# Decode of two attention-and-MLP layers: the two halves of a head's score rows gathered in one bank, and the last query weights loaded first from two queues

## The chip, the cores and the metric

The kernel runs on one core of a Trainium2 chip. A core has a matrix engine (TensorE, PE in the profile, with its weight loads shown apart as PEld), a vector engine (VectorE, DVE), a scalar engine (ScalarE, ACT), a general one (GpSimd, POOL) and a queue engine (SyncE, SP), each with its own instruction stream, and 16 DMA engines that move data from the chip's main memory into its working memory (SBUF). PE writes into eight banks of accumulator memory (PSUM); DVE and ACT copy from there. The metric is the device time of one execution in microseconds, as the median of several executions; less is better.

## The reference

Eight rows x of 448 numbers, one per batch entry, go twice through an attention block A and an MLP block B, with the same caches and weights in both layers:

```python
x = x + _A_ref(_layernorm(x), A_k_cache, A_v_cache, A_wq, A_wo)
x = x + _B_ref(_layernorm(x), B_w1, B_w2, B_w3, B_w4)
x = x + _A_ref(_layernorm(x), A_k_cache, A_v_cache, A_wq, A_wo)
x = x + _B_ref(_layernorm(x), B_w1, B_w2, B_w3, B_w4)
```

In A, x times `wq` gives 16 query heads of 256 numbers; each of the 8 key-value heads serves two of them. For each batch entry and key-value head there are 4096 keys and 4096 values of 256 numbers in bf16 (2 MB each): scores q.k / 16, a softmax over the 4096 positions, the weighted sum of the values, and `wo` on the 16 results together. In B, a first part (`w1`, `w2`) shifts along a sequence of length one, so that nothing of it is left and x1 = x; the rest is x1 + gelu(layernorm(x1) w3) w4, with 1792 hidden numbers.

## The kernel before, in words

**Order of the work.** The whole program is written as a list of operations, each with an engine, a modelled duration, the keys that it reads and writes, the PSUM banks that it touches, and a priority. `Plan.schedule` (L156) places them one by one in modelled time: on each engine, among the operations that are ready, the one of lowest priority number. `Plan.synchronise` turns the dependences into semaphore waits, and each engine then runs its own list strictly in order. Where PE would stand idle in the model, `filler` (L1672) puts in matmuls that keep its clock up (L1679 in the profile). An operation with engine "ev" is an eviction that the schedule gives to DVE or ACT, whichever can take it first.

**Loads.** All loads but one result go out on SP's queue (`dma`, L623, and `load`, L649). SP's priorities are of their own: a load of keys or values has its running number 0, 1, 2, ..., and a weight load made by `dma_once` (L629) with `at` has 4 * at - 0.5. So `at = 0` goes ahead of all keys, and `at = 2` (7.5) behind the first eight quarters of key and value tiles. Keys and values pass through one buffer `kv` of 30 slots; a slot holds a quarter of a head's keys or values (512 KB), and adjacent free slots can be filled by one load of up to four quarters (2048 KB). SP waits until the operation that last read a slot is done (L643 in the waits of SP).

**Heads.** `front(layer, b, h)` makes the scores and the softmax of a head, `back(layer, b, h)` the weighted sum of values and the part of `wo`. In front, each quarter u of the keys that was loaded anew is transposed by PE in two pieces (`transpose_piece`, L1464; transposes at L1476) into one of four banks psT0 to psT3, which go round by `next_bank` and `tcount`, and copied back over its own slot by DVE (L1407) or ACT (L1408). Of the 8 key heads the five last, and some quarters of their values, stay in the buffer from the first layer to the second (`KEEP_K`), where their keys are not transposed again.

**Scores by rows.** 13 of the 16 head passes of a batch entry (7 of the first layer, 6 of the second; not the last head, nor the first one of the second layer) score "by rows": the queries, 32 columns, stand still in PE and the keys stream through it, 512 at a time. `score_rows` (L1365, matmuls at L1374) scores two quarters: four groups of 32 output rows, for the four half quarters, each in two passes c = 0, 1 over the even and odd elements of a head. `turn_rows` (L1383) copies that bank to a tile `sr` (512 columns in bf16, by DVE at L1387 or ACT at L1388), and four matmuls (L1398) turn it so that positions lie along partitions, and pick the two rows that belong to head h out of each group. This happens twice a head, for quarters 0 and 1 and for quarters 2 and 3, each time in a bank of its own and through the one tile `sr`. The other passes score with the keys as the stationary side (L1136). All scores of a head land in 64 columns of bank psM; then sS (L1204), the maximum (L1209, L1211, L1215), the exponential (L1221), the sum (L1225, L1227).

**The queries** lie in four tiles: `q1b` and `q2T`, two each (by the parity of b), for the first and the second layer, 16 columns for c = 0, 16 for c = 1 and 16 of zeros. The first layer's are made for all batch entries at the start by `first_queries` (L1558), 128 matmuls at L892 that need all of wq and wqx. The second layer's are made head by head, between one head's scores and the next one's, by `second_queries` (L1522, L892 and L1527), which use psM as well.

**Query weights.** `wq` has 448 rows. Three loads of 128 rows each (1024 KB) fill `wq_sb`. Of the last 64 rows, columns 0 to 2047 go to partitions 0 to 63 of `wqx_sb`, and columns 2048 to 4095 to partitions 64 to 127, with a load of 256 KB each.

**Around it.** `mid` (L1506) runs the MLP of one row between the layers and makes the first queries of the second layer; the heads of the first layer for the next batch entry run beside it. For one batch entry (`MLP_ROW`, b = 5) `with_first_results` lends one of the four psT banks to an MLP of six rows. The last quarters of the last head's keys in the first layer stay in the four psT banks until the second layer takes them (`hold`, `held_banks`).

Of the kernel before, what the change touches and what calls it, by code (L numbers as in the profile page):

```python
# [6 lines left out]
P = 128  # L7
B = 8
D = 448
HKV = 8  # L10
DH = 256
# [461 lines left out]
def bass_interleave_layers__gqa_block_cached__mixer_s_mlp__decode_kernel(  # L473
# [43 lines left out]
    w4_sb = sb("w4_sb", [P, 14 * D], bf)  # L517
    ident_f = sb("ident_f", [P, P], f32)
    ident_b = ident_f[:, :].bitcast(bf)[:, 1:2 * P:2]
    xT = sb("xT", [P, NC5, B], bf)  # L520

# [10 lines left out]
    ymk = acc[0]  # L532
    cs_q = sb("cs_q", [P, 32], f32)
    cs_h = sb("cs_h", [P, 14], f32)
# [9 lines left out]
    kh = sb("kh", [P, 1024], bf)  # L544
    q2T = [sb(f"q2T{i}", [P, 48], bf) for i in range(2)]
    cursor[0] = (cursor[0] + 31) // 32 * 32
# [22 lines left out]
    x_row = over("x_row", [B, NC5 * P], bf, w4_sb)  # L569
    NR, NO, NS = 6, 2, 2  # L570
    pT = [sb(f"pT{i}", [P, 32, 2], bf) for i in range(NR)]
    pm = [sb(f"pm{i}", [P, 2], f32) for i in range(NS)]
# [7 lines left out]

    sS = [sb(f"sS{i}", [P, 64], bf) for i in range(NS)]
    oS = sb("oS", [P, 2, DH], bf)
    o_last = over("o_last", [P, G], bf, oS)
# [507 lines left out]
    done = {}  # L1091

    def first_q(b, prio):
        for c in range(2):
            dv(lambda v, c=c: v.tensor_copy(
                q1b[b % 2][:, 16 * c:16 * c + 16].rearrange("p (h j) -> p h j", j=2),
                psM[:, Q1 + b:Q1 + 32 * B:B].rearrange("p (h j c) -> p h c j", j=2, c=2)[:, :, c, :]),
               rd=["q1"], wr=[("q1b", b % 2, c)], banks=[M], prio=prio)

    def front(layer, b, h, prio=None):  # L1100
# [8 lines left out]
        if layer == 0:  # L1109
            def rhs(c):  # L1110
                return q1b[b % 2][:, 16 * c + 2 * h:16 * c + 2 * h + 2]
            qall = q1b[b % 2]
            qk = [("q1b", b % 2, 0), ("q1b", b % 2, 1)]
        else:
            def rhs(c):
                return q2T[b % 2][:, 16 * c + 2 * h:16 * c + 2 * h + 2]
            qall = q2T[b % 2]
            qk = [("q2", b % 2, h)]
        ks = dict(kept_k)
        fresh = [u for u in range(4) if u not in ks and not (layer and h == HALF)]  # L1120
# [30 lines left out]
        for u in range(4):  # L1151
# [79 lines left out]
    def back(layer, b, h):  # L1231
# [132 lines left out]

    def score_rows(qs, qall, keys, prio):  # L1365


        bank = next_bank()

        def mm(t):  # L1370
            last = None
            for c in range(2):
                for g in range(4):
                    last = t.matmul(psT[bank][32 * g:32 * g + 32, :], qall[:, 16 * c:16 * c + 32],  # L1374
                                    slot_ap(qs[g // 2], g % 2 * 1024, 1024)[:, c:1024:2], start=(c == 0),
                                    stop=(c == 1), skip_group_check=True, tile_position=(0, 32 * g))
            return last
        o = plan.op("pe", mm, (0.47, 0.92, 1024, 8), "scr", rd=keys, wr=[("psT", bank)],
                    banks=[("T", bank)], prio=prio and prio + len(plan.ops))
        o.tbank = bank  # L1380
        return o

    def turn_rows(half, h, bank, par, prio):  # L1383

        def ev(e):
            if e is nc.vector:
# [3 lines left out]
                prio=prio and prio + len(plan.ops)).tbank = bank  # L1390

        picks = ident_b.rearrange("p (g c) -> p g c", g=4)[:, :, 2 * h:2 * h + 2]

        def mm(t):
            last = None
            for k in range(4):
                a = SB + 32 * half + 8 * k
                last = t.matmul(psM[:, a:a + 8], sr[:, k * P:(k + 1) * P], picks, start=True, stop=True)  # L1398
            return last
        plan.op("pe", mm, (0.17, 0.17, 32, 4), "scturn", rd=SR + ["ident_f"],  # L1400
                wr=[("sc", par, x) for x in range(2 * half, 4)], banks=[M], prio=prio and prio + len(plan.ops))

# [119 lines left out]
    def second_queries(b, h, prio):  # L1522

        q, src = q2T[b % 2], x2c[b % 2]
        pe(lambda t: q_mms(t, range(4 * h, 4 * h + 4), lambda kc: src[:, kc, 0:1], psM, SC,
                           1, QW), 16, rd=[("x2", b)] + WQ, wr=["psM"], banks=[M], prio=prio, width=QW)
        dv(lambda v: v.scalar_tensor_tensor(  # L1527
            q[:, 0:32].rearrange("p (c x) -> p c x", c=2)[:, :, 2 * h:2 * h + 2],
            cs_q[:, 4 * h:4 * h + 4].rearrange("p (c j) -> p c j", c=2), mom2[b % 2][:, 2:3],
# [209 lines left out]
```

## Time and profile before

| | |
|---|---|
| median of 3 executions | 1093.52 us (1092.39 to 1094.42) |
| the profiled execution, its own time | 1095.86 us |
| its span, first to last instruction | 1094.1 us |
| mean granted PE clock | 0.933 |
| busy: PE, DVE, ACT, POOL | 948.4, 665.9, 335.0, 98.0 us |
| read from main memory | 434.18 MB, 397 GB/s over the span |

The profile is that of one execution. Its span leaves out what lies before the first and after the last instruction, here 1.8 us. "Busy" counts an engine's instructions; what an engine waited for stands in the lists of waits. Lines such as L1387 are those of the listing above.

### The profile page before, as it was taken

The page shows a single profiled execution, that of the slowest core. Times are in us where ns is not written, and L with a number is a line of the kernel's source. Part 1 is how long each engine was busy: PE and PEld are TensorE (multiplying, and loading weights), DVE is VectorE, ACT ScalarE, POOL GpSimd, SP SyncE. Part 2 cuts the span into 40 slices and gives each one's busy share as a digit, 9 for nine tenths or more (in the row PEclk, how much of TensorE's full clock was granted, in tenths as well). Part 3 has the DMA queues.
Part 4 walks back from the last instruction along what each step waited for, and adds up shares of the span by engine and source line. Part 5 has one row for each costly group of instructions (what it writes and reads, how often), then busy time and mean ns, then how long its engine had stood idle before and what let it go on. Part 6 is the DMA issues. An engine that isn't in the chain of part 4 may idle for free.

```text
span 1094.1 us, 34653 instructions
## 1 busy us (share of the span) xinstructions
PE 948.4 (87%) x15414; PEld 636.6 (58%) x15414; DVE 665.9 (61%) x2004; ACT 335.0 (31%) x935; POOL 98.0 (9%) x281
## 2 busy tenths in 40 slices
PE   4889888898988989888988889888898998999886
PEld 3556555565556655666556565566555765566554
DVE  3457445675656756666567675667555765566565
ACT  0234123341334303343133322334133440343131
POOL 0001000010100101011010101001010000111010
PEclk9899899997999969999799998999899997999896
DMA  9999999999999999999999999999999999999892
GB/s 333 409 424 421 391 403 425 426 418 375 410 424 427 412 390 392 425 424 415 372 425 425 424 404 390 425 425 420 398 380 427 424 417 381 396 426 410 310 412 120
DMA packets 60417, 436.43 MB, mean 399 GB/s; under 512 B 6494, under 2 KB 9708, under 8 KB 39276
## 3 DMA queue, kind: packets, MB, share of 16 engines
q1 hardware_dynamic: 60260, 434.22, 97.5%
q8 instruction: 121, 1.98, 0.7%
q14 instruction: 28, 0.23, 0.1%
q10 hardware_dynamic: 8, 0.00, 0.0%
HBM read 434.18 MB, written 0.01 MB: 397 GB/s over the span
## 4 chain that ended last, share of the span: by engine, by line
DMA 57%; PE 31%; DVE 6%; ACT 2%; issue 2%; SPq 1%; POOL 0%; POOLq 0%; DVEq 0%
DMA kv<-in_A_v_cache_dram 39%; DMA kv<-in_A_k_cache_dram 15%; PE psT L1476 8%; PE psP L1257 8%; PE psT L1374 4%; PE psM L1136 3%; PE psR L1307 2%; PE psM L892 2%; DMA wqx_sb<-in_A_wq_dram 2%; DMA w_sb<-in_B_w_dram 1%; PE psM L1054 1%; DVE kv L1407 1%; ACT pT L1221 1%; SPq L626 1%; ACT kv L1408 1%
## 5 line engine op out<-in xcount | busy, mean ns | idle before, releaser
L1476 PE MATMUL psT<-ident_f,kv 128*128 128x128 f32 x2752 | 391.5, 283 | 27.0 <-DMA kv<-in_A_k_cache_dram 25.0
L1476 PEld LDWEIGHTS psT<-ident_f,kv 128*128 128x128 f32 x2752 | 296.7, 142 | 111.8 <-issue 69.6
L1407 DVE COPY kv<-psT 128x512 f32<-128x512 f32 x388 | 265.7, 690 | 135.3 <-PE psT L1476 131.4
L1408 ACT COPY kv<-psT 128x512 f32<-128x512 f32 x332 | 193.3, 586 | 437.3 <-PE psT L1476 340.1
L1257 PE MATMUL psP<-kv,pT 128*2 128x256 bf16 x4096 | 185.8, 293 | 36.4 <-DMA kv<-in_A_v_cache_dram 28.8
L1387 DVE CAST sr<-psT 128x512 bf16<-128x512 f32 x157 | 108.4, 691 | 73.6 <-PE psT L1374 60.2
L1257 PEld LDWEIGHTS psP<-kv,pT 128*2 128x2 bf16 x4096 | 76.1, 82 | 90.0 <-DMA kv<-in_A_v_cache_dram 44.3
L1211 POOL PARTITION_ALL_REDUCE gm<-pm x128 | 45.4, 355 | 773.2 <-DVE pm L1209 768.4
L1374 PE MATMUL psT<-kv,q1b 128*32 128x512 bf16 x896 | 72.5, 394 | 17.9 <-ACT kv L1408 14.9
L1221 ACT ACTIVATE pT<-sS,nb,fac 128x32 bf16<-128x32 bf16 x128 | 52.6, 417 | 106.9 <-DVE nb L1215 106.9
L1271 DVE CAST oS<-psP 128x256 bf16<-128x256 f32 x128 | 53.7, 419 | 45.8 <-PE psP L1257 45.3
L1307 PE MATMUL psR<-wo_sb,oT 128*1 128x448 bf16 x444 | 67.4, 387 | 3.5 <-DVE oT L1287 3.1
L1225 POOL PARTITION_ALL_REDUCE Db<-rs x128 | 51.0, 398 | 195.3 <-ACT pT L1221 195.3
L1374 PE MATMUL psT<-kv,q2T 128*32 128x512 bf16 x768 | 60.3, 397 | 3.4 <-DVE kv L1407 2.0
L1398 PEld LDWEIGHTS psM<-ident_f,sr 128*128 128x128 bf16 x832 | 42.5, 97 | 30.7 <-DVE sr L1387 16.5
L1398 PE MATMUL psM<-ident_f,sr 128*128 128x8 bf16 x832 | 52.4, 170 | 7.9 <-DVE sr L1387 6.5
L1221 ACT ACTIVATE pT<-sS,nb 128x32 bf16<-128x32 bf16 x128 | 40.8, 326 | 57.7 <-DVE nb L1215 57.6
L1273 DVE TENSOR_TENSOR oS<-psP,oS 128x256 bf16<-128x256 f32 x128 | 54.2, 424 | 3.5
L1281 PEld LDWEIGHTS psP<-sel,oS 128*128 128x128 bf16 x512 | 24.4, 99 | 39.5 <-DVE oS L1273 29.2
L1204 DVE CAST sS<-psM 128x64 bf16<-128x64 f32 x128 | 27.8, 217 | 29.5 <-PE psM L1136 20.2
L1281 PE MATMUL psP<-sel,oS 128*128 128x2 bf16 x512 | 32.2, 167 | 14.1 <-DVE oS L1273 13.3
L1388 ACT CAST sr<-psT 128x512 bf16<-128x512 f32 x51 | 29.8, 585 | 42.2 <-PE psT L1374 37.9
(197 smaller groups left out, 853.0 us busy)
## 6 DMA issues: line engine op xcount, KB each, us to landing
kv<-in_A_k_cache_dram SPq DMA_DIRECT2D x69, 2048.0 KB, 20.8
kv<-in_A_v_cache_dram SPq DMA_DIRECT2D x53, 2048.0 KB, 17.8
kv<-in_A_v_cache_dram SPq DMA_DIRECT2D x187, 512.0 KB, 7.5
kv<-in_A_v_cache_dram SPq DMA_DIRECT2D x21, 1024.0 KB, 11.1
kv<-in_A_k_cache_dram SPq DMA_DIRECT2D x40, 512.0 KB, 8.1
kv<-in_A_k_cache_dram SPq DMA_DIRECT2D x10, 1536.0 KB, 15.6
kv<-in_A_v_cache_dram SPq DMA_DIRECT2D x5, 1536.0 KB, 12.2
wo_sb<-in_A_wo_dram SPq DMA_DIRECT2D x1, 3584.0 KB, 45.6
```

The costliest lines, as they stand in the source:

```text
L1221: return a.activation(pT[nr][:, :, :].rearrange("p i j -> p j i")[:, jj, :], sview[:, jj, :], ACT.Exp, bias=nb[nm][:, jj:jj + 1], scale=sc ...
L1257: last = t.matmul(ps[g4:g4 + 2, PV0:PV0 + DH], pT[nr][:, k, :], slot_ap(q, s * 256, 256), start=(i < 4), stop=(i >= 28), skip_group_check= ...
L1271: plan.op("dve", lambda v: v.tensor_copy(oS[:, 0, :], po), 0.36, "o", rd=[("pv", par, x) for x in range(4)], wr=["oS0"], banks=[bk], prio=hi)
L1273: plan.op("dve", lambda v: v.tensor_tensor(oS[:, 1, :], po, oS[:, 0, :], ALU.subtract), 0.36, "o", rd=["oS0"] + [("pv", par, x) for x in r ...
L1281: last = t.matmul(ps[:, PV1 + 2 * c:PV1 + 2 * c + 2], oS[:, w, c:DH:2], sel[:, :], start=(w == 0), stop=(w == 1))
L1307: last = t.matmul(psR[r:r + 1, 0:D], oT[no][:, i % 2, i // 2:i // 2 + 1], wo_sb[:, a:a + D], start=(k == 1 and i < 2), stop=(k == turn_at ...
L1374: last = t.matmul(psT[bank][32 * g:32 * g + 32, :], qall[:, 16 * c:16 * c + 32], slot_ap(qs[g // 2], g % 2 * 1024, 1024)[:, c:1024:2], sta ...
L1387: return e.tensor_copy(sr[:, :], psT[bank][:, :])
L1398: last = t.matmul(psM[:, a:a + 8], sr[:, k * P:(k + 1) * P], picks, start=True, stop=True)
L1407: return e.tensor_copy(dst, psT[bank][:, :])
L1408: return e.copy(dst, psT[bank][:, :])
L1476: last = t.transpose(psT[bank][:, s * P:(s + 1) * P], src, ident_f[:, :])
```

## The change

Two edits stand in one diff, and the tiles move a little for them.

**One copy a head.** The four query tiles become one tile `qz` of 272 columns: for each layer and each parity of b 64 columns, in which 16 zeros, the 16 queries of c = 0, 16 zeros and the 16 queries of c = 1 follow each other, with 16 zeros at the end. A window of 32 columns that begins at the queries of c holds them in its first 16 columns and zeros in the others; a window that begins 16 columns earlier holds the zeros first. So the first half of a head's keys scores into the upper 16 rows of each group of 32, and adds zero to the lower ones; the second half the other way round, in the same bank. The bank is taken before the first half (`held_banks.add`), kept out of the round of banks meanwhile, and given back with the one copy that follows the second half. The four turning matmuls then pick four columns of each group, 16 in all, instead of two.

**The wqx loads.** The load for partitions 0 to 63 gets `at = 0.05` (priority -0.3), behind x and ahead of the first keys, on SP; the one for partitions 64 to 127 is issued by ACT, as its first operation. The wq loads keep their place. Both need semaphores of their own, as before.

```diff
+    qz = sb("qz", [P, 272], bf)
...
-    q1b = [sb(f"q1b{i}", [P, 48], bf) for i in range(2)]
-    q2T = [sb(f"q2T{i}", [P, 48], bf) for i in range(2)]
...
-        for q in q1b + q2T:
-            gp.memset(q[:, :], 0.0)
+        gp.memset(qz[:, :], 0.0)
...
+    def at_q(layer, b, c):
+
+        return 128 * layer + 64 * (b % 2) + 16 + 32 * c
...
-                o = score_rows([ks[u - 1], ks[u]], qall, qk + full + [("s", ks[u - 1], 0), ("s", ks[u - 1], 1)], prio)
-                turn_rows(u // 2, h, o.tbank, par, prio)
+                if u == 1:
+                    rbank = next_bank()
+                    held_banks.add(rbank)
+                o = score_rows([ks[u - 1], ks[u]], u // 2, lambda c, half: at_q(layer, b, c) - 16 * half, rbank,
+                               qk + full + [("s", ks[u - 1], 0), ("s", ks[u - 1], 1)], prio)
+                if u == 3:
+                    turn_rows(h, rbank, par, prio)
...
-                    k = 16 * (u // 2) + 4 * (s % 4) + 2 * (u % 2) + s // 4 if in_rows else i
+                    k = 8 * (s % 4) + 4 * (u // 2) + 2 * (u % 2) + s // 4 if in_rows else i
...
-    def score_rows(qs, qall, keys, prio):
-        bank = next_bank()
+    def score_rows(qs, half, window, bank, keys, prio):
...
             for c in range(2):
+                a = window(c, half)
                 for g in range(4):
-                    last = t.matmul(psT[bank][32 * g:32 * g + 32, :], qall[:, 16 * c:16 * c + 32],
-                                    slot_ap(qs[g // 2], g % 2 * 1024, 1024)[:, c:1024:2], start=(c == 0),
-                                    stop=(c == 1), skip_group_check=True, tile_position=(0, 32 * g))
+                    last = t.matmul(psT[bank][32 * g:32 * g + 32, :], qz[:, a:a + 32],
+                                    slot_ap(qs[g // 2], g % 2 * 1024, 1024)[:, c:1024:2],
+                                    start=(half == 0 and c == 0), stop=(half == 1 and c == 1),
+                                    skip_group_check=True, tile_position=(0, 32 * g))
...
-        o.tbank = bank
+        if half == 0:
+            o.tbank = bank
...
-    def turn_rows(half, h, bank, par, prio):
+    def turn_rows(h, bank, par, prio):
...
-        picks = ident_b.rearrange("p (g c) -> p g c", g=4)[:, :, 2 * h:2 * h + 2]
+        held_banks.remove(bank)
+        picks = ident_b.rearrange("p (g a x) -> p a g x", g=4, a=2)[:, :, :, 2 * h:2 * h + 2]
...
-                a = SB + 32 * half + 8 * k
-                last = t.matmul(psM[:, a:a + 8], sr[:, k * P:(k + 1) * P], picks, start=True, stop=True)
+                a = SB + 16 * k
+                last = t.matmul(psM[:, a:a + 16], sr[:, k * P:(k + 1) * P], picks, start=True, stop=True)
...
-        dma_once("wqx", [(wqx_sb[0:64, :], A_wq[384:D, 0:2048], 1 << 19),
-                         (wqx_sb[64:P, :], A_wq[384:D, 2048:4096], 1 << 19)], ["wqx0", "wqx1"], 2)
+        dma_once("wqx", [(wqx_sb[0:64, :], A_wq[384:D, 0:2048], 1 << 19)], ["wqx0"], 0.05)
+        s_wqx = nc.alloc_semaphore("s_wqx1")
+        plan.op("act", lambda a: a.dma_start(wqx_sb[64:P, :], A_wq[384:D, 2048:4096]), 0.1, "wqx1",
+                wr=["wqx1"], prio=0, dma=(s_wqx, 16))
```

The tiles cs_q, kh, pT, sS and oS are laid out earlier in SBUF; what reads or writes the query tiles uses `qz` and `at_q` instead.

More of the change, by code (lines that the diff above doesn't have):

```diff
@@ L518, in bass_interleave_layers__gqa_block_cached__mixer_s_mlp__decode_kernel @@
     ident_f = sb("ident_f", [P, P], f32)
+    NR, NO, NS = 6, 2, 2
     ident_b = ident_f[:, :].bitcast(bf)[:, 1:2 * P:2]
+    cs_q = sb("cs_q", [P, 32], f32)
+    qz = sb("qz", [P, 272], bf)
+    kh = sb("kh", [P, 1024], bf)
+    pT = [sb(f"pT{i}", [P, 32, 2], bf) for i in range(NR)]
+    sS = [sb(f"sS{i}", [P, 64], bf) for i in range(NS)]
+    oS = sb("oS", [P, 2, DH], bf)
     xT = sb("xT", [P, NC5, B], bf)
@@ L532, in bass_interleave_layers__gqa_block_cached__mixer_s_mlp__decode_kernel @@
     ymk = acc[0]
-    cs_q = sb("cs_q", [P, 32], f32)
     cs_h = sb("cs_h", [P, 14], f32)
@@ L569, in bass_interleave_layers__gqa_block_cached__mixer_s_mlp__decode_kernel @@
     x_row = over("x_row", [B, NC5 * P], bf, w4_sb)
-    NR, NO, NS = 6, 2, 2
-    pT = [sb(f"pT{i}", [P, 32, 2], bf) for i in range(NR)]
     pm = [sb(f"pm{i}", [P, 2], f32) for i in range(NS)]
@@ L579, in bass_interleave_layers__gqa_block_cached__mixer_s_mlp__decode_kernel @@
     xs = over("xs", [P, G], f32, pT[0])
-    sS = [sb(f"sS{i}", [P, 64], bf) for i in range(NS)]
-    oS = sb("oS", [P, 2, DH], bf)
     o_last = over("o_last", [P, G], bf, oS)
@@ L1095, in first_q @@
             dv(lambda v, c=c: v.tensor_copy(
-                q1b[b % 2][:, 16 * c:16 * c + 16].rearrange("p (h j) -> p h j", j=2),
+                qz[:, at_q(0, b, c):at_q(0, b, c) + 16].rearrange("p (h j) -> p h j", j=2),
                 psM[:, Q1 + b:Q1 + 32 * B:B].rearrange("p (h j c) -> p h c j", j=2, c=2)[:, :, c, :]),
@@ L1109, in front, with rhs @@
         if layer == 0:
-            def rhs(c):
-                return q1b[b % 2][:, 16 * c + 2 * h:16 * c + 2 * h + 2]
-            qall = q1b[b % 2]
             qk = [("q1b", b % 2, 0), ("q1b", b % 2, 1)]
         else:
-            def rhs(c):
-                return q2T[b % 2][:, 16 * c + 2 * h:16 * c + 2 * h + 2]
-            qall = q2T[b % 2]
             qk = [("q2", b % 2, h)]
+        def rhs(c):
+            a = at_q(layer, b, c) + 2 * h
+            return qz[:, a:a + 2]
         ks = dict(kept_k)
@@ L1396, in mm @@
             for k in range(4):
-                a = SB + 32 * half + 8 * k
-                last = t.matmul(psM[:, a:a + 8], sr[:, k * P:(k + 1) * P], picks, start=True, stop=True)
-            return last
-        plan.op("pe", mm, (0.17, 0.17, 32, 4), "scturn", rd=SR + ["ident_f"],
-                wr=[("sc", par, x) for x in range(2 * half, 4)], banks=[M], prio=prio and prio + len(plan.ops))
+                a = SB + 16 * k
+                last = t.matmul(psM[:, a:a + 16], sr[:, k * P:(k + 1) * P], picks, start=True, stop=True)
+            return last
+        plan.op("pe", mm, (0.17, 0.17, 64, 4), "scturn", rd=SR + ["ident_f"],
+                wr=[("sc", par, x) for x in range(4)], banks=[M], prio=prio and prio + len(plan.ops))
     def evacuate(i, pc, bank):
@@ L1522, in second_queries @@
     def second_queries(b, h, prio):
-        q, src = q2T[b % 2], x2c[b % 2]
+        src = x2c[b % 2]
         pe(lambda t: q_mms(t, range(4 * h, 4 * h + 4), lambda kc: src[:, kc, 0:1], psM, SC,
@@ L1527, in second_queries @@
         dv(lambda v: v.scalar_tensor_tensor(
-            q[:, 0:32].rearrange("p (c x) -> p c x", c=2)[:, :, 2 * h:2 * h + 2],
+            qz[:, at_q(1, b, 0):at_q(1, b, 0) + 64].rearrange("p (c x) -> p c x", c=2)[:, :, 2 * h:2 * h + 2],
             cs_q[:, 4 * h:4 * h + 4].rearrange("p (c j) -> p c j", c=2), mom2[b % 2][:, 2:3],
```

1 line of the change is left out of this document (removed).

## The prediction

> **What bounds the kernel now.** I read the page first, then the table of stretches, then the waits of the load queue, then the timeline at the three places where loading is not at full pace.
>
> ```profile
> span 1094.1 us, 34653 instructions
> ...
> PE 948.4 (87%) x15414; PEld 636.6 (58%) x15414; DVE 665.9 (61%) x2004; ACT 335.0 (31%) x935; POOL 98.0 (9%) x281
> ...
> q1 hardware_dynamic: 60260, 434.22, 97.5%
> ...
> DMA 57%; PE 31%; DVE 6%; ACT 2%; issue 2%; SPq 1%; POOL 0%; POOLq 0%; DVEq 0%
> ```
>
> The packets of the load queue fill 97.5% of the span on all 16 DMA engines, and 57% of the chain that ended last is loading. PE at 87% is next. So a microsecond of copying or matmul saved is worth nothing where loading runs at full pace; it counts only where loading pauses. The table of stretches (busy time of PE, PEld, DVE, ACT, POOL, then clock, DMA share and GB/s at the end of the row) shows where:
>
> ```profile
> 2.50:20.80 18.30, 6.76 (x69) 5.71 (x69) 6.26 (x27) 0.58 (x1) 0.28 (x1) 1.00 1.00 399
> 20.80:25.60 4.80, 3.50 (x19) 1.90 (x19) 2.07 (x3) 0.58 (x1) 0.00 (x0) 1.00 1.06 220
> 25.60:44.00 18.40, 15.50 (x246) 9.68 (x247) 5.86 (x15) 3.60 (x9) 0.78 (x2) 0.81 1.01 423
> 300.00:350.00 50.00, 43.13 (x595) 29.18 (x594) 31.18 (x78) 19.32 (x49) 4.17 (x11) 1.00 1.01 425
> 412.00:421.00 9.00, 8.55 (x191) 4.92 (x195) 4.94 (x19) 1.43 (x8) 1.13 (x4) 1.00 0.95 325
> 672.00:680.00 8.00, 7.16 (x172) 4.10 (x167) 5.08 (x18) 1.81 (x8) 1.45 (x4) 1.00 0.99 340
> 799.00:808.00 9.00, 7.85 (x199) 5.01 (x194) 6.11 (x20) 2.28 (x9) 1.30 (x4) 1.00 0.89 319
> 929.00:937.00 8.00, 7.10 (x178) 4.53 (x175) 4.97 (x17) 2.33 (x10) 1.51 (x4) 1.00 0.94 339
> 1070.00:1094.00 24.00, 14.55 (x357) 9.77 (x349) 12.94 (x54) 3.08 (x11) 1.15 (x3) 0.71 0.21 81
> ```
>
> Full pace is 425 GB/s (300 to 350). Three kinds of place fall short: 20.8 to 25.6, at 220 GB/s although the engines are counted as busy 1.06 times over; a dip of 8 or 9 us in four of the eight batches, 319 to 340; and the tail, where nothing is left to load.
>
> **The change part by part.** *The query weights.* The start, from the timeline:
>
> ```profile
> 0.72 0.75 SPq L626 DMA_DIRECT2D x_row<-in_A_x_dram  x2
> 1.52 0.83 SPq L643 DMA_DIRECT2D kv<-in_A_k_cache_dram  x2
> 2.39 1.65 SPq L626 DMA_DIRECT2D wq_sb<-in_A_wq_dram  x3
> 4.09 1.20 SPq L626 DMA_DIRECT2D wqx_sb<-in_A_wq_dram  x2
> ...
> 20.21 0.58 ACT L1408 COPY kv<-psT 128x512 f32<-128x512 f32 x1 [18.21 <-PE psT L1476]
> ...
> 26.21 0.22 PE L892 MATMUL psM<-yb,wq_sb 128*128 128x8 bf16 x3 [1.09 <-DMA wqx_sb<-in_A_wq_dram]
> ```
>
> The two wqx loads, 256 KB for 64 partitions each, are the last that the first queries wait for (26.21). Ahead of them loading flows at 399 and behind them at 423; around their landing the rate halves. In 4.8 us, 4.8 x 220 = 1056 KB moved, which at 425 take 2.5 us: 2.3 us are lost. My reading: a load of 64 partitions reaches only half of the paths into the memory, and two such loads one behind the other on one queue use first one half, then the other. Afterwards the second one goes out on ACT's queue while SP sends the first, so both halves should be filled together. The costs: the first key load is issued one issue later, 1.20 / 2 = 0.6 us, while the weights themselves keep the engines at work; ACT sits idle for 18.21 us before its first copy at 20.21. Bounds: +0.6 us (the loads stay slow and the keys start late) and -2.9 us (all the loss gone, and ACT's issue fills 0.6 us of the empty start). I take **-2.0**, near the row that measures the loss. It carries to the end since loading behind it runs at 423. The first queries then wait for wq instead, some 3 to 5 us earlier than 26.21; I count that at nothing, as the stream from 25.6 to 44 is full anyway.
>
> The Trainium skill speaks against this part: "DMA: Bandwidth & Descriptors", section "Rules for kernel authors", says of two transfers to disjoint partition halves not to bother, because they serialize on the same 16 engines, whichever queue issues them. By that rule the sum would lack its -2.0. The trace agrees that the engines are shared, but not that they are the limit in this stretch: they count as busy while moving 220 of 425.
>
> *One copy a head.* The groups concerned:
>
> ```profile
> L1387 DVE CAST sr<-psT 128x512 bf16<-128x512 f32 x157 | 108.4, 691 | 73.6 <-PE psT L1374 60.2 <-PE psM L1398 10.9
> L1388 ACT CAST sr<-psT 128x512 bf16<-128x512 f32 x51 | 29.8, 585 | 42.2 <-PE psT L1374 37.9 <-PE psM L1398 4.3
> L1398 PE MATMUL psM<-ident_f,sr 128*128 128x8 bf16 x832 | 52.4, 170 | 7.9 <-DVE sr L1387 6.5 <-DVE oT L1287 0.4 <-ACT sr L1388 0.3
> ```
>
> 157 + 51 = 208 copies are two for each of 104 heads scored by rows. 104 go: (108.4 + 29.8) / 2 = 69 us of DVE and ACT. Of 832 turning matmuls 416 go with their weight loads, 52.4 / 2 = 26 us of PE; the rest write 16 columns instead of 8, which at 170 ns for so narrow a one I price at nothing. The score matmuls stay as many and as wide. Nearly all of this lies beside loading at full pace and is worth nothing there: the cover is the DMA row above. Four memsets on POOL, which is 9% busy, become one: nothing.
>
> It counts in the dips. They lie where second-layer heads with kept keys are scored by rows one after another, from about 412 on:
>
> ```profile
> 414.70 1.59 PE L1374 MATMUL psT<-kv,q2T 128*32 128x512 bf16 x16
> ...
> 415.89 0.69 DVE L1387 CAST sr<-psT 128x512 bf16<-128x512 f32 x1
> ...
> 417.55 0.26 PE L1398 MATMUL psM<-ident_f,sr 128*128 128x8 bf16 x4
> ...
> 417.85 0.69 DVE L1387 CAST sr<-psT 128x512 bf16<-128x512 f32 x1 [1.14 <-PE psM L1398]
> ...
> 419.25 0.21 DVE L1204 CAST sS<-psM 128x64 bf16<-128x64 f32 x1
> ...
> 420.41 0.57 PEld L1374 LDWEIGHTS psT<-kv,q2T 128*32 128x32 bf16 x16 [0.29 <-DVE q2T L1527]
> 420.41 1.09 PE L1374 MATMUL psT<-kv,q2T 128*32 128x512 bf16 x16
> ...
> 422.33 0.69 DVE L1387 CAST sr<-psT 128x512 bf16<-128x512 f32 x1 [0.20 <-PE psM L1398]
> ...
> 423.72 0.21 DVE L1204 CAST sS<-psM 128x64 bf16<-128x64 f32 x1
> ```
>
> Both halves are scored by 414.70 + 1.59 = 416.29, but the second copy waits until the first is turned (1.14 us idle behind L1398), as both use the one tile sr; only then come the second turn, sS, the next head's queries (L1527) and its scores at 420.41. From the second copy's start to sS are 419.25 - 417.85 = 1.40 us. With one copy it starts right after the scores, at about 416.35, and sS at 417.75: 1.5 us earlier. For the next head, scores end at about 420.41 + 1.09 = 421.50, sS would come at 421.56 + 1.39 = 422.95 instead of 423.72: 0.8 us. Mean 1.1 us a head. Who waits is SP; its own waits, from 926 to 948:
>
> ```profile
> SPq L643 <- PE psT L1374: 8.7, 2, 6.0
> SPq L643 <- PE psM L1136: 5.2, 3, 4.0
> ```
>
> 8.7 us go to slots that the row scores free, 5.2 to the heads without rows just ahead, which the change leaves as they are. Against 425 the four dips lose 9 x (1 - 325/425) = 2.1, 1.6, 2.2 and 1.6, together 7.5 us. Bounds: 0 (the wait passes to L1136 whole) and -7.5. One head's 1.1 us in each would be -4.4; since part of each dip belongs to L1136, I take **-3.5**.
>
> What the change adds is a wait: the score bank is held from the first half until the copy after the second, so the transposes of the second half turn in three banks, and behind them PE's queue stands. What that could cost is the first rival; in the sum I price it at nothing, covered by PE's idle time in full-pace stretches.
>
> *The tail.* The last heads end as PE lets them:
>
> ```profile
> 1070.80 0.69 DVE L1387 CAST sr<-psT 128x512 bf16<-128x512 f32 x1 [2.02 <-PE psT L1374]
> ...
> 1071.58 0.26 PE L1398 MATMUL psM<-ident_f,sr 128*128 128x8 bf16 x4
> ...
> 1073.80 0.58 ACT L1388 CAST sr<-psT 128x512 bf16<-128x512 f32 x1 [0.85 <-PE psT L1374]
> ```
>
> Of the last head the copy at 1070.80 and the turn at 1071.58 go; the copy at 1073.80 stays. The turn's 0.26 us is in PE's queue ahead of the work that ends last, and the copy may free DVE for the next. Bounds 0 and -1.0 (0.69 + 0.26); I take **-0.5**.
>
> Sum: -2.0 - 3.5 - 0.5 = -6.0 us. The span of 1094.1 becomes 1088.1; the profiled execution took 1095.86 with what lies around the span and becomes 1089.9. The median of the runs shown is 1093.52, 2.3 below that execution, and becomes **1087.5**.
>
> **The rivals.**
>
> *The held bank makes it slower.* Transposes now hardly wait for copies:
>
> ```profile
> L1476 PE MATMUL psT<-ident_f,kv 128*128 128x128 f32 x2752 | 391.5, 283 | 27.0 <-DMA kv<-in_A_k_cache_dram 25.0 <-ACT kv L1408 0.8 <-DVE kv L1407 0.2
> ```
>
> 0.8 + 0.2 us in the whole run with four banks. From 300 to 350 PE is idle 50 - 43.13 = 6.9 us, and a head with new keys and values (2 x 4096 x 256 in bf16, 4.19 MB, at 425) takes 9.9 us, so 1.4 us of idle time a head; the lost turn adds 0.26. Three banks decide from a stall of about 1.6 us a head on, more than two copies of 0.69. There are 80 heads by rows with new keys (56 in the first layer, 24 in the second), so each 0.1 us above that costs 8 us. At 1.75 us: +12, less the 2.0 of the start: 1103.5.
>
> *Nothing to gain.* The weights serialize as the skill's rule has it, and the dips are passed to L1136 or to the values that PE consumes. The time stays at 1093.5, at most 0.5 less.
>
> *The start alone.* The dips keep their length but the weights flow: -2.0 and -0.5, 1091.0.
>
> *The dips close altogether.* -2.9 - 7.5 - 1.0, and 2 more where smaller dips in other batches close: 1080.
>
> **How the numbers follow.** About 0.2%, 2.2 us, is what a measurement of this kernel can tell from no change: faster means below 1091.3, slower above 1095.7. Forecast 0.48; dips closed 0.10; start alone 0.14, of which 0.10 below 1091.3; nothing to gain 0.14; held bank 0.14. So faster 0.68, same 0.18, slower 0.14. The range runs from 1080.5, just short of closed dips, to 1095.5, above no gain, with the 0.6 of the late keys and the order of loads that is worked out anew; it leaves out the held bank and about half of the closed dips, 2 in 10.
>
> **What would show it.** In the changed profile: 104 copies into sr, not 208, and 416 turning matmuls. Stretches of 220 GB/s around 21 to 25 gone, and none so slow in the first 6 us; L892 starting between 21 and 23.5. In the dips of the later batches the time from a head's last score to sS near 1.4 us, SP's waits on row scores shorter, and GB/s nearer to 390. Wrong would be: transposes waiting for copies by tens of microseconds (the held bank); wqx still crawling, only elsewhere; or dips as deep as now with SP waiting on other lines.

## The result, and the profile after

| | before | after |
|---|---|---|
| median, measured side by side | 1092.04 us (1088.91 to 1094.42, 6 executions) | 1086.41 us (1083.13 to 1091.09, 6 executions) |
| ratio to before | | 0.9948, 95% interval 0.9924 to 0.9971 |
| profiled execution, its span | 1095.86, 1094.1 us | 1083.66, 1081.5 us |

The changed kernel is 5.7 us faster (0.52%); the forecast was 6.0 faster. The two profiled executions lie further apart than the medians, because that of before was a long one of its kind and that of after a short one. So each reading of the traces below needs kernels that were timed many times beside it.

The page of after, the rows that answer to those of before:

```profile
span 1081.5 us, 33945 instructions
...
PE 944.7 (87%) x15116; PEld 650.5 (60%) x15116; DVE 600.1 (55%) x1896; ACT 338.3 (31%) x939; POOL 98.3 (9%) x278
...
q1 hardware_dynamic: 58740, 433.95, 98.0%
...
L1392 DVE CAST sr<-psT 128x512 bf16<-128x512 f32 x58 | 40.1, 691 | 29.4 <-PE psT L1377 29.1
...
L1686 PE MATMUL psP<-ident_f 128*128 128x256 bf16 x331 | 51.7, 283 | 0.0
```

DVE lost 66 us of work, and the load queue fills its share as before. PE lost little, although 416 turning matmuls are gone: the schedule puts its fillers (L1686) where PE would stand idle, 71.9 us of them by the groups of after against 56.4 in before. The groups of after, the other two rows of the new copy and its turn:

```profile
L1393 ACT CAST sr<-psT 128x512 bf16<-128x512 f32 x46 | 27.0, 586 | 50.3 <-PE psT L1377 48.5 <-PE psM L1403 1.8
L1403 PE MATMUL psM<-ident_f,sr 128*128 128x16 bf16 x416 | 26.8, 176 | 3.9 <-DVE sr L1392 3.2 <-ACT sr L1393 0.6
```

58 + 46 = 104 copies and 416 turns, as the change says. Sixteen columns take 176 ns where eight took 170: nothing, as priced.

The stretches of after at the start (busy time of each engine, clock, DMA share, GB/s):

```profile
2.50:20.80 18.30, 5.67 (x61) 5.21 (x62) 5.05 (x25) 0.71 (x2) 0.28 (x1) 1.00 1.01 391
20.80:25.60 4.80, 4.36 (x35) 3.54 (x34) 3.46 (x5) 2.07 (x4) 0.00 (x0) 1.00 1.02 435
25.60:44.00 18.40, 16.67 (x277) 10.77 (x281) 7.03 (x20) 4.54 (x15) 1.53 (x4) 0.91 1.00 417
```

The stretch of 220 GB/s is gone. It gives (435 - 220) x 4.8 = 1032 KB; ahead of it (399 - 391) x 18.3 = 146 KB are lost, and behind it (423 - 417) x 18.4 = 110 KB. What is left, 776 KB, at 425 is 1.8 us, beside the forecast of 2.0.

The dips of after, each where it now lies, behind a stretch at full pace:

```profile
300.00:350.00 50.00, 44.85 (x549) 30.90 (x547) 29.72 (x75) 18.15 (x47) 4.17 (x11) 0.97 1.01 426
407.00:416.00 9.00, 7.97 (x192) 5.55 (x196) 5.17 (x20) 1.97 (x9) 1.64 (x5) 1.00 1.02 388
666.00:674.00 8.00, 7.63 (x181) 4.49 (x170) 4.96 (x19) 1.81 (x8) 1.51 (x4) 1.00 1.01 374
792.00:801.00 9.00, 8.09 (x192) 5.02 (x192) 6.02 (x20) 3.11 (x14) 1.70 (x5) 1.00 0.98 359
921.00:929.00 8.00, 7.29 (x184) 4.57 (x183) 5.07 (x18) 2.33 (x10) 1.70 (x5) 1.00 0.96 350
```

388, 374, 359 and 350 GB/s, where before had 325, 340, 319 and 339. Against 425 these four lose 4.6 us, those of before 7.5. That looks like the second term of the forecast coming true. A reader who stops here would take the whole sum for shown. It isn't, as the single parts show.

### The profile page after: what moved, and what is told of

Its sections match the earlier page's. It is cut to its first block, busy times and chain, and to the rows that moved or that the text cites. A ratio compares the mean times of both kernels' runs of the same rounds, so it can differ in the third digit from the quotient of the medians.

```text
span 1081.5 us, 33945 instructions
## 1 busy us (share of the span) xinstructions
PE 944.7 (87%) x15116; PEld 650.5 (60%) x15116; DVE 600.1 (55%) x1896; ACT 338.3 (31%) x939; POOL 98.3 (9%) x278
## 4 chain that ended last, share of the span: by engine, by line
DMA 52%; PE 37%; DVE 6%; issue 2%; ACT 1%; SPq 0%; POOL 0%; POOLq 0%; DVEq 0%
DMA kv<-in_A_k_cache_dram 32%; DMA kv<-in_A_v_cache_dram 19%; PE psT L1481 14%; PE psP L1261 7%; PE psT L1377 5%; PE psM L1135 3%; PE psR L1311 2%; PE psM L890 2%; DMA w3x_sb<-in_B_w_dram 1%; DVE oS L1277 1%; PE psP L1686 1%; DVE oS L1275 1%; DVE kv L1412 1%; PE psP L1285 1%; PE psM L1052 1%
## 5 line engine op out<-in xcount | busy, mean ns | idle before, releaser
L1481 PE MATMUL psT<-ident_f,kv 128*128 128x128 f32 x2752 | 381.6, 286 | 28.5 <-DMA kv<-in_A_k_cache_dram 26.5
L1481 PEld LDWEIGHTS psT<-ident_f,kv 128*128 128x128 f32 x2752 | 307.7, 145 | 109.6 <-issue 59.8
L1412 DVE COPY kv<-psT 128x512 f32<-128x512 f32 x377 | 258.4, 691 | 187.7 <-PE psT L1481 182.7
L1261 PE MATMUL psP<-kv,pT 128*2 128x256 bf16 x4096 | 181.2, 293 | 20.8 <-DMA kv<-in_A_v_cache_dram 18.4
L1377 PE MATMUL psT<-kv,qz 128*32 128x512 bf16 x1664 | 132.5, 394 | 4.3 <-ACT kv L1413 2.0
L1261 PEld LDWEIGHTS psP<-kv,pT 128*2 128x2 bf16 x4096 | 83.3, 83 | 66.2 <-DMA kv<-in_A_v_cache_dram 31.2
L1377 PEld LDWEIGHTS psT<-kv,qz 128*32 128x32 bf16 x1664 | 34.1, 95 | 39.2 <-issue 10.9
L1392 DVE CAST sr<-psT 128x512 bf16<-128x512 f32 x58 | 40.1, 691 | 29.4 <-PE psT L1377 29.1
L1686 PE MATMUL psP<-ident_f 128*128 128x256 bf16 x331 | 51.7, 283 | 0.0
L1135 PEld LDWEIGHTS psM<-qz,kv 128*128 128x128 bf16 x1344 | 41.9, 100 | 14.8 <-issue 5.4
L1135 PE MATMUL psM<-qz,kv 128*128 128x48 bf16 x1344 | 48.5, 188 | 1.4 <-DVE qz L1532 0.3
```

What stands on the lines that cost most here:

```text
L1135: last = t.matmul(ps[:, SB + 2 * i:SB + 2 * i + 2 * REP], a()[:, c:256:2], bcast(rhs(c), REP, 1), start=(c == 0), stop=(c == 1))
L1377: last = t.matmul(psT[bank][32 * g:32 * g + 32, :], qz[:, a:a + 32], slot_ap(qs[g // 2], g % 2 * 1024, 1024)[:, c:1024:2], start=(half == ...
L1412: return e.tensor_copy(dst, psT[bank][:, :])
L1481: last = t.transpose(psT[bank][:, s * P:(s + 1) * P], src, ident_f[:, :])
L1686: return t.matmul(dst, ident_b, bcast(ident_b[:, 0:n // 4], 4, 1), start=True, stop=True)
```

## The experiments

The theory on trial is that of the prediction: the loads are worth 2.0 us at the start, the shorter chain of a row head 3.5 in the dips and 0.5 at the end. Against it stand: the loads are worth it all; the dips hang on something other than that chain; the rule of the Trainium skill, by which the loads are worth nothing; and, once both parts were seen alone, that an order of work laid out anew is itself worth microseconds. All ratios are to before, measured beside it, with 95% intervals; us are the ratio's share of 1092.

| kernel | ratio | interval | us |
|---|---|---|---|
| loads alone | 0.9955 | 0.9937 to 0.9972 | -4.9 |
| one copy alone | 0.9997 | 0.9978 to 1.0016 | -0.3 |
| both loads first on SP | 0.9982 | 0.9963 to 1.0001 | -2.0 |
| one load, old place | 0.9979 | 0.9961 to 0.9998 | -2.3 |
| loads, old order | 0.9981 | 0.9967 to 0.9995 | -2.1 |
| old loads, new order | 0.9989 | 0.9976 to 1.0002 | -1.2 |
| before, laid out anew | 1.0008 | 0.9993 to 1.0023 | +0.9 |
| loads, laid out anew | 0.9987 | 0.9971 to 1.0004 | -1.4 |
| after, laid out anew | 0.9993 | 0.9977 to 1.0008 | -0.8 |
| after, copy in eight | 0.9956 | 0.9940 to 0.9971 | -4.8 |
| after, first scores twice | 1.0206 | 1.0182 to 1.0229 | +22.5 |
| after, two banks left | 1.0008 | 0.9984 to 1.0032 | +0.9 |

**Each part alone.** The first kernel is before with the diff's lines on wqx and no others; the second is after with before's lines on wqx.

> The kernel before with the wqx edit alone. Mine (two loads of 64 partitions side by side fill both halves of the paths): no stretch of 220 GB/s around 20.8 to 25.6 us and none as slow in the first 6 us; the first queries start 3 to 5 us earlier than 26.21; time -2.0 us (-0.2%), between -2.9 and +0.6. Rival (they serialize wherever they stand): a slow stretch of about 5 us appears near the start, time 0. Rival (all of the gain comes from the start): -5.6 us, the whole of what was measured.

> The changed kernel with the old wqx loads. Mine: -4.0 us (-0.37%), with the dips after the batch entries' row scores at about 390 GB/s in place of 319 to 340, and the stretch of 220 GB/s around 21 to 25 us still there. Rival (the copies are hidden everywhere): 0 to -0.5 us. Rival (the held bank costs time and the loads make up for it): above 0.

The loads alone gave 4.9 us, the copy alone 0.3 (between 2.4 faster and 1.7 slower). The 4.0 us that the prediction gave to the copy are outside that interval. The stretches of the copy alone, the start and the four dips, and then the dips of the loads alone:

```profile
20.80:25.60 4.80, 4.37 (x32) 3.15 (x31) 3.19 (x5) 1.76 (x3) 0.00 (x0) 1.00 1.09 232
```

```profile
412.00:421.00 9.00, 8.46 (x214) 6.02 (x218) 5.50 (x21) 2.05 (x9) 1.73 (x5) 1.00 0.90 331
673.00:681.00 8.00, 7.76 (x189) 4.96 (x187) 5.38 (x19) 1.81 (x8) 1.51 (x4) 1.00 0.87 302
801.00:810.00 9.00, 8.29 (x193) 5.01 (x195) 5.98 (x21) 2.82 (x14) 1.92 (x5) 1.00 0.89 316
931.00:939.00 8.00, 7.22 (x175) 4.44 (x177) 5.24 (x19) 2.30 (x12) 1.51 (x4) 1.00 1.00 379
```

```profile
406.00:415.00 9.00, 8.14 (x195) 5.04 (x198) 5.50 (x20) 2.21 (x10) 1.55 (x5) 1.00 1.03 409
666.00:674.00 8.00, 7.18 (x183) 4.40 (x179) 4.77 (x18) 1.49 (x7) 1.11 (x3) 1.00 0.96 353
793.00:802.00 9.00, 7.44 (x184) 4.74 (x188) 5.39 (x19) 1.74 (x7) 1.51 (x4) 1.00 1.03 401
923.00:931.00 8.00, 7.21 (x177) 4.40 (x175) 5.02 (x17) 2.33 (x10) 1.51 (x4) 1.00 0.98 350
```

With the one copy and the old loads the dips are as deep as before (331, 302, 316, 379, together 7.5 us lost against 425); with two copies and the new loads they are as shallow as in after (409, 353, 401, 350, together 3.6). So the shallow dips of after aren't the copy's doing. The slow start, 232, stays with the old loads. In the loads alone the first queries start at 25.5, not 3 to 5 us ahead of 26.21.

**What makes the loads slow.** Before, with both 64-partition loads ahead of the keys but on SP alone, one behind the other; and before, with one load of 128 partitions in their old place behind wq, which brings the same bytes but lays the rows into other partitions, so that the queries come out as other numbers:

```diff
-                         (wqx_sb[64:P, :], A_wq[384:D, 2048:4096], 1 << 19)], ["wqx0", "wqx1"], 2)
+                         (wqx_sb[64:P, :], A_wq[384:D, 2048:4096], 1 << 19)], ["wqx0", "wqx1"], 0.05)
```

```diff
+        dma_once("wqx", [(wqx_sb[:, :], A_wq[384:D, :].rearrange("k (h n) -> (k h) n", h=2), 1 << 20)], ["wqx0"], 2)
```

> The kernel before with both wqx loads ahead of the first keys, but one behind the other on SP. Mine (the pattern, not the place, makes them slow): the first keys are held up and the 2.3 us are lost at the start, between 2 and 8 us; time -0.5 to +0.6 us. Rival (the place alone matters): as with the two queues, no slow stretch, -2 us.

> The kernel before with one load of 128 partitions for all of wqx, at the old place in SP's queue; the rows of the weights then lie in other partitions than the products take them from, which changes numbers and no instruction. Mine (64 partitions are what is slow): 20.8 to 25.6 us at 400 GB/s or more, first queries about 2 us earlier than 26.21, time -2.3 us. Rival (the place, behind the other weights, is slow): 220 GB/s still, time 0.

The two stretches of interest in each, first both loads on SP, then the one load; last the front stretch of before and of after:

```profile
2.00:8.00 6.00, 0.00 (x0) 0.00 (x0) 0.60 (x4) 0.01 (x1) 0.00 (x0) 1.00 0.75 235
...
20.80:25.60 4.80, 3.24 (x20) 1.68 (x18) 1.38 (x2) 0.59 (x1) 0.00 (x0) 1.00 1.04 440
```

```profile
2.00:8.00 6.00, 0.00 (x0) 0.00 (x0) 0.60 (x4) 0.00 (x1) 0.00 (x0) 1.00 0.96 342
...
20.80:25.60 4.80, 3.96 (x45) 2.60 (x45) 2.08 (x3) 0.61 (x2) 0.00 (x0) 1.00 1.05 445
```

```profile
2.00:8.00 6.00, 0.00 (x0) 0.00 (x0) 0.59 (x4) 0.01 (x1) 0.00 (x0) 1.00 0.93 331
```

```profile
2.00:8.00 6.00, 0.00 (x0) 0.00 (x0) 0.59 (x4) 0.62 (x1) 0.00 (x0) 1.00 1.02 328
```

The front stretch holds the start of the stream too: with no half-wide load in it, before has 331 GB/s there and the one load 342. One behind the other, the two loads are slow there as well, 235. On two queues after has 328 and the loads alone 284. One load over all partitions flows at 445 in the very place where two took 220.

Counted from the packets, the first 12 MB have arrived 2.6 us earlier than in before with the one load, 1.1 us earlier with both on SP, and 1.7 to 2.3 us earlier in the eight kernels with the loads on two queues; the three other kernels with the old loads lie within 0.2 us of before. So the half rate belongs to two half-wide loads in a row, and one wide load cures it without the front place or a second queue. Two half-wide loads side by side in mid-stream were not run, nor one half-wide load alone, so the number of loads isn't parted from their width.

Total time doesn't part these two kernels: both on SP came out at -2.0, as the rival said, with an interval that reaches no change, and in both kernels the order of the other work is laid out anew as well. It is the stretch that tells them apart.

**Loads or order?** The loads alone gave more than the start's stretch can hold. An edit of one load lets the schedule lay out the whole program anew, so the two were parted. The third kernel keeps before's order on every engine and moves only the two loads in the finished lists; the fourth takes the order of the loads alone and moves the loads back behind wq on SP:

```diff
+    w0, w1 = [o for o in sp if o.name == "wqx"]
...
+    w1.eng = "act"
...
+    sp.insert(at, w0)
+    act.insert(0, w1)
```

> The new wqx loads, with every other instruction on every engine in the order of the kernel before (the order is worked out with the old loads, and the two loads are moved afterwards). Theory A (the loads give only what they save at the start; the rest of the 5 us that they brought alone came from the order that was worked out anew): -1.7 to -2.5 us. Theory B (an earlier start of the first queries or of the loading is worth more than its own length later): -5 us as with the loads alone.

> The old wqx loads at their old place in SP's queue, with all other instructions in the order of the kernel that has the new loads alone. Theory A (the order brings the rest): -2.5 to -3 us. Theory B (the loads bring all of it): 0.

With the order kept, the loads are worth 2.1 us (0.5 to 3.6). The new order without them gave 1.2 (its interval includes nothing), where theory A expected 2.5 to 3 and theory B 0; this run alone decides nothing. To see what an order is worth, the modelled time of the copy to sr was changed by 0.02 us in before, in the loads alone, and in after. It lays all out anew and alters no work of the kernel, only the number of fillers and which evictions DVE takes and which ACT:

```diff
-        plan.op("ev", ev, {"dve": 0.71, "act": 0.6}, "evr", rd=[("psT", bank)], wr=SR, banks=[("T", bank)],
+        plan.op("ev", ev, {"dve": 0.73, "act": 0.62}, "evr", rd=[("psT", bank)], wr=SR, banks=[("T", bank)],
```

> The kernel before, in which only the modelled time of the copies into sr is raised by 0.02 us, so that the order is worked out anew and nothing else changes. It measures what a new order alone can do: theory A says differences of 2 us or more either way are ordinary; theory B says within 1 us of before.

> The two query-weight loads side by side, copies as before, the planner's modelled eviction time 0.73/0.62 instead of 0.71/0.60, which lays the order out anew and changes nothing else. Theory A (the loads are worth about 2 us, the rest of loads_only's 4.9 us is the order that it happened to get): 1 to 4 us faster than before, within 2 us of loads_old_order. Theory B (the loads themselves are worth 5 us): 5 us faster than before, as loads_only.

> After, with the planner's modelled eviction time 0.73/0.62 instead of 0.71/0.60, which lays the order out anew and changes nothing else. Theory A (loads 2 us, one copy nothing, the rest the order): 1 to 4 us faster than before, about the same as loads_replanned. Theory B (loads 5 us): 5 us faster than before. If the one copy were worth 4 us as predicted: 4 us faster than loads_replanned.

The three came out at +0.9, -1.4 and -0.8 us. Before moved by less than 1 us, as theory B said. But the loads lose 3.5 us of their 4.9, and after loses 4.9 of its 5.7: the intervals of after (0.9924 to 0.9971) and of after laid out anew (0.9977 to 1.0008) don't meet, though both run the same instructions but for fillers and the share of DVE and ACT in the evictions. So theory A held for these two, at its lower edge: after laid out anew came out 0.2 below its 1 to 4. Only one other order of each kernel was tried, so how far orders scatter isn't known.

Three pairs of kernels now differ in the copies alone: the copy alone against before (-0.3), after against the loads alone (-0.8), and the same two laid out anew (+0.6). Each is known to 2 or 3 us either way, their mean of -0.2 to some 1.5. The 4.0 us of the prediction show in none.

**Does the row head's chain matter at all?** After, in its own order, with the one copy cut into eight of 64 columns:

```diff
+            for i in range(0, 512, 64):
+                d, s = sr[:, i:i + 64], psT[bank][:, i:i + 64]
+                last = e.tensor_copy(d, s) if e is nc.vector else e.copy(d, s)
```

> The changed kernel, in its own order, with the one copy a head cut into eight of 64 columns. Eight copies of the kind that sS is (0.217 us each) take up to 1.7 us in place of 0.69, so a head's way from its scores to sS grows by up to 1.0 us again. Mine as predicted (the dips are as long as that way): +2 to +4 us against the changed kernel, so about -0.2% against before. Rival (the way of the heads by rows doesn't set the dips; the loads that refill the queue hang on the heads without rows before them): 0 against the changed kernel, -0.5% against before.

The groups of that kernel:

```profile
L1393 DVE CAST sr<-psT 128x64 bf16<-128x64 f32 x464 | 66.1, 214 | 31.9 <-PE psT L1377 31.7
L1393 ACT CAST sr<-psT 128x64 bf16<-128x64 f32 x368 | 47.2, 250 | 47.3 <-PE psT L1377 45.5 <-PE psM L1404 1.8
```

66.1 + 47.2 = 113.3 us for 104 heads are 1.09 a head, where 40.1 + 27.0 = 67.1 were 0.65: the copying is 0.44 us longer in every row head. The chain from the last score to sS, which other waits share, is 0.25 us longer: 1.55 us against 1.30 in after and 1.76 in before (medians over the 104 heads, counted from the traces). The time is that of after, 0.9956 beside 0.9948, but known to about 3 us either way only. At the prediction's own rate, 3.5 us for 1.1 us a head, 0.25 us would cost 0.8, which this run can't tell from nothing. It leans against the expected 2 to 4 us; it doesn't show that the chain is free. What happened in the dips themselves says more; it stands with the reasons below.

**What do the dips hang on?** After in its own order, but the second-layer heads that are scored without rows, which lie just ahead of the row heads, issue each pair of score matmuls twice into the same bank:

```diff
-                    for c in range(2):
+                    for c in (0, 1, 0, 1) if layer else (0, 1):
```

> After with its order, but in the second layer the heads that are scored without rows (ahead of the row heads) issue each score matmul pair twice, the same result into the same bank: about 1 us more TensorE time a head, and each first key load of the next item is released that much later. Theory 'the dips hang on the heads without rows ahead of the row heads': SP's key loads wait for these heads' scores, so the dips grow and the kernel is 5 to 20 us slower than after. Rival, the prediction's 'the chain of the row heads sets the dips': 0 to 1 us slower than after.

It came out 28 us slower than after by the two ratios, some 4 either way: the rival's 0 to 1 is refuted, and the theory's 5 to 20 was too small. First the two groups of these scores in that kernel (one reads the keys from the tile kh) and a wait of SP's queue, then the same in after:

```profile
L1135 PE MATMUL psM<-qz,kv 128*128 128x48 bf16 x2240 | 73.1, 187 | 7.0 <-issue 5.8
...
L1135 PE MATMUL psM<-qz,kh 128*128 128x48 bf16 x320 | 12.7, 187 | 0.6 <-ACT kh L1421 0.3
```

```profile
SPq L642 <- PE psM L1135: 94.1, 41, 8.6
```

```profile
L1135 PE MATMUL psM<-qz,kv 128*128 128x48 bf16 x1344 | 48.5, 188 | 1.4 <-DVE qz L1532 0.3 <-issue 0.3
...
L1135 PE MATMUL psM<-qz,kh 128*128 128x48 bf16 x192 | 8.7, 183 | 2.9 <-ACT kh L1421 2.5 <-DVE kh L1420 0.3
```

```profile
SPq L642 <- PE psM L1135: 73.1, 39, 6.4
```

So 896 + 128 = 1024 matmuls in 16 heads added 24.6 + 4.0 = 28.6 us of PE (28 ns each, since they overlap; 1.8 us a head instead of the 1 us that the expectation assumed), and the time grew by as much: at this place PE's work counts one for one. The row heads behind start later by it too, so this run prices PE's work here and doesn't show by itself that the row heads' chain is free. SP waits 21 us longer for these scores. In the stretch where it stands the rate falls to 180 GB/s:

```profile
418.00:420.00 2.00, 1.85 (x70) 1.62 (x66) 0.29 (x2) 0.00 (x0) 0.00 (x0) 1.00 0.48 180
420.00:422.00 2.00, 1.10 (x36) 0.82 (x40) 0.20 (x2) 0.00 (x0) 0.35 (x1) 1.00 0.89 186
```

And the chain that ended last in after points the same way without any experiment: it goes through these heads to the key load behind them, and no copy of row scores is in it here. (In before it does pass one, the 0.69 us at 417.85; in the copy alone the two evictions to oS, 0.44 and 0.43 us, stand at that place instead.)

```profile
402.27 1.23 PE psM L1135 x32
403.58 0.43 PE psM L1135 x16
404.03 0.23 DVE sS L1208
...
406.63 0.53 ACT kh L1421 x2
407.21 0.79 PE psM L1135 x24
408.01 6.31 DMA kv<-in_A_k_cache_dram
```

What makes PE late at this place wasn't varied. In before and in the copy alone its granted clock is 0.50 from 396 to 406, just ahead of this dip; how much of the dip that is stays open.

**Is the held bank dear?** After with a second bank held from the first half to the copy, which leaves two for the transposes, the order laid out anew:

```diff
+                    xbank = next_bank()
+                    held_banks.add(xbank)
...
+                    held_banks.remove(xbank)
```

> After with one more bank of the transposes held from the first half of the scores to the one copy, so that the transposes of the second half turn in two banks instead of three; the order is laid out anew. Mine: idle TensorE of about 1.4 us a head takes up the waiting, 0 to 5 us slower than after. Rival, the held bank limits the kernel: 12 us slower than after or more.

It came out 6.5 us slower than after, between the two expectations; against after laid out anew it is 1.6 slower (about 3 either way). Waiting for copies, the transposes and the row scores in it, then the transposes in after:

```profile
L1484 PE MATMUL psT<-ident_f,kv 128*128 128x128 f32 x2752 | 391.9, 285 | 36.4 <-DMA kv<-in_A_k_cache_dram 28.2 <-DVE kv L1415 4.0 <-ACT kv L1416 2.1
...
L1380 PE MATMUL psT<-kv,qz 128*32 128x512 bf16 x1664 | 134.5, 398 | 17.8 <-DVE kv L1415 8.9 <-ACT kv L1416 5.9 <-DVE qz L1535 0.5
```

```profile
L1481 PE MATMUL psT<-ident_f,kv 128*128 128x128 f32 x2752 | 381.6, 286 | 28.5 <-DMA kv<-in_A_k_cache_dram 26.5 <-ACT kv L1413 1.2 <-DVE kv L1412 0.4
```

One held bank costs the transposes 1.6 us of waiting in the whole run, against 1.0 before; even two cost 6.1. The row scores wait 14.8 us for copies here and 3.0 in after, but 18.4 in before, where no bank was held, so that figure isn't the bank's price.

## Why the prediction was right, and where it was wrong

The sum was nearly exact, -6.0 against -5.7, but by luck: one of its three terms stood, and a cause that it didn't have made up the rest.

- **Start, -2.0: right** in size, and in what made the loads slow. 1.8 us by the stretches, 2.1 with the order kept. The rule of the Trainium skill ("DMA: Bandwidth & Descriptors", section "Rules for kernel authors"), that transfers to disjoint partition halves serialize wherever they are issued, would have made it 0; the measured 2.1 decides against that. The same row of the rules asks for one 128-partition transfer instead, and with that the trace agrees: 445 GB/s. One behind the other the halves do crawl, at 220 in mid-stream, and at 235 in front, where 331 flow without them. On two queues the front stretch has 279 to 328, so some of the loss can come back there. The 435 of after is the rate of a stretch that no longer holds these loads. Only argued: that the half rate comes from the paths into the memory.
- **First queries between 21 and 23.5: wrong.** L890 of after first ran at 27.1, L892 of before at 26.21. Its data were there, the last of the wq loads since 24.1; PE's order had transposes and five fillers ahead of it. No cost of it can be seen: loading runs at 417 there.
- **Dips, -3.5: the step failed that turned the shorter chain of a row head into loading time.** The chain itself shrank where and as it was said. From the last score to sS, the first row head of each dip takes 2.95, 2.83, 2.81 and 2.36 us in before and 1.33, 1.33, 1.25 and 1.33 in the copy alone, the second one 2.22, 2.28, 2.49 and 2.59 against 1.71, 1.72, 2.18 and 1.27 (counted from the traces): 1.05 us a head, beside the 1.1 of the prediction. But the dips of the copy alone lose 7.5 us, as those of before do. PE used the time: of the 8.55 us that it is busy in the row that the prediction quotes, 412 to 421, 1.01 are fillers, at 418.06 and 418.71, while the second copy and its turn are waited for; the copy alone has no filler there and 8.46 us of PE. Loading did not use it. The fillers of before and of the copy alone in that row (busy time of PE and PEld, clock, DMA share, GB/s):

```profile
412.00:421.00 9.00, 1.01 (x3) 0.22 (x3) 1.00 0.95 325
```

```profile
412.00:421.00 9.00, 0.00 (x0) 0.00 (x0) 1.00 0.90 331
```

What stayed is the wait of SP on the heads without rows just ahead. Its longest in the four dips is 4.7, 4.0, 4.1 and 4.0 us in before and 4.0 in each in the copy alone, here from 926 to 948, to be held against the prediction's 5.2:

```profile
SPq L642 <- PE psM L1135: 4.8, 3, 4.0
```

Longer scores of these heads cost one for one. A wait that stays there is the prediction's own lower bound, "the wait passes to L1136 whole"; it saw that "part of each dip belongs to L1136" and still took nearly half of the loss. That a dip's GB/s rose in after was no proof either way: it rose without the copy as well. Nor were SP's waits on row scores: in windows that lie alike to the dips they are 7.9, 10.2, 9.6 and 8.7 us in before, 8.5, 11.4, 11.3 and 2.6 in after, and 11.2, 6.5, 6.5 and 4.6 in the copy alone. The last and the first window of after, to be held against the prediction's 8.7 (926 to 948) and before's 7.9 (400 to 430):

```profile
SPq L642 <- PE psT L1377: 2.6, 1, 2.6
```

```profile
SPq L642 <- PE psT L1377: 8.5, 2, 4.6
```

- **Tail, -0.5: mis-sized, and not seen in the time.** From the landing of the last values to the end of the span, counted from the packets, the five one-copy kernels with three banks take 13.5 to 13.9 us and the eight with two copies 15.0 to 18.1: about 3 us less, outside the bounds of 0 and 1.0. Yet the copy alone isn't 3 us faster; in its profile the last values land at 1077.4, in that of before at 1076.3. Where loading loses this stays open, since single executions of one kernel differ by more (1087.5 to 1095.6 for the copy alone).
- **The held bank:** rightly priced at nothing, as far as the waits for copies show it.
- **The order laid out anew: not in the prediction**, except as a margin of the range. The same edits with another order gave 0.8 us instead of 5.7, so the order is the larger part of what was measured. Which places of the order matter isn't settled: the extra loss lies in dips spread over the batches, at other places in each profile.

So of 5.7 us some 2 are the loads' and none can be shown for the one copy (the copy alone allows 2.4 at most); most of the remainder is shown to go with the order.

## What to carry to other kernels

Where a schedule is computed, an edit is two edits, itself and the new order; before believing a gain of half a per cent, lay the same edit out a second time by a change that alters no work, and run the old order with the edit in it. A shorter chain of latencies is worth nothing by itself: ask what waits for its end, and whether that is what holds the bottleneck. Here PE used the time and loading, which waited elsewhere, did not. So read the longest waits of the loading queue first, and take the fillers off an engine's busy share before reading it as work. And look for loads that fill only half of the partitions one behind another; one wide load cured it in place, and the two halves on two queues at the start gained nearly as much.

## What the runs showed of the hardware

- Two 64-partition loads in a row on one queue hold the rate in mid-stream at 220 GB/s (before) and 232 (the copy alone), while the DMA engines count as 1.06 and 1.09 busy. The busy share alone doesn't show that loading is slow; the GB/s beside it does.
- The mean granted clock didn't go with the time: 0.923 in the faster profile of after, 0.933 in that of before.
- Eight narrow copies in place of one wide one cost less than their number: each takes 214 ns on DVE for 64 columns against 691 for 512, and 250 against 586 on ACT, but they overlap, and the eight take 1.09 us a head together.
